# Decay columns made in the first batch, two more pairs transposed by DMA, and the last result in halves: a fused attention and MLP kernel

## The chip, the core and the metric

The kernel runs on one core of a Trainium2 chip. The metric is the time of one execution on the device, in microseconds (us). A core has TensorE (PE, with weight loads shown apart as PEld), VectorE (DVE), ScalarE (ACT), GpSimd (POOL) and SyncE (SP). SP computes nothing here; it issues most of the DMAs, one after the other and in program order. The profile gives one busy share for the core's 16 DMA engines, for all queues together.

## The reference, cut to what matters

Attention over 8 batches of 8 heads with 576 rows of 64 columns. The scores have a causal mask and a decay made from a running sum of `s`. Then an MLP with a hardswish between two matrices.

```python
scores = scale * np.matmul(q, k.transpose(0, 1, 3, 2))
s_pos = np.maximum(s, 0.0)
cum = np.cumsum(s_pos, axis=-1)
bias = -(cum[:, :, :, None] - cum[:, :, None, :])
scores = np.where(causal, -1e9, scores + np.minimum(bias, 0.0))
attn = softmax(scores)                       # written out in the original
x = np.matmul(attn, v)                       # then (B*S, H*D)
h = x @ w_in
out = (h * np.clip(h + 3.0, 0.0, 6.0) / 6.0) @ w_out
```

## The kernel before, where the change touches it

Heads go in 32 pairs. Scores need q and k transposed (the 64 columns on the partitions), with the decay as additional rows under them. Two ways exist side by side. Pairs below `PTD` are transposed on TensorE and copied by the DVE, and get their decay rows from a scratch tensor in memory (`load_aug`). Pairs from `PTD` on are laid out in SBUF with decay *columns* beside q and k, and one DMA transposes the whole.

```python
    PTD = 10
# ...
    def decay_columns():                      # all three parts, once, before pair 7
        for i in range(3):
            pD = psum.tile([128, NTR, NH], F16, tag="S", bufs=3, name="pD")
            for t in range(NTR + 1):          # ten small transposes
                nc.tensor.matmul(out=pD[r0:r1, j, :], lhsT=kaug[:, i, c:c + r1 - r0], ...)
            for r0, r1, j0, j1, h in (...):   # four DVE copies, eight for i == 0
                nc.vector.tensor_copy(out=dec[r0:r1, j0:j1, i, :], in_=src)
# ...
    def cast_columns(p):                      # POOL: q, k and the decay columns into xb
        nc.gpsimd.tensor_copy(out=..., in_=qk_f.pop(p))
        nc.gpsimd.tensor_copy(out=x[:, NTR:2 * NTR, D:D + 3], in_=dec[:, :, 0:3, p])
        nc.gpsimd.tensor_copy(out=x[:, 0:NTR, D + 3:D + 4], in_=dec[:, :, 3:4, p])

    def transpose_dma(p):                     # on the SP queue
        nc.sync.dma_start(out=qkT[:, p % NS, ...], in_=xb[:, p % 2]..., transpose=True)

    def load_pair(p):                         # also on the SP queue
        load_qk(p, nc.sync)
        load_v(p, nc.sync)
        if p < PTD:
            load_aug(p, nc.sync)
# ...
    def block0_tasks(p):                      # pairs 4 to 7, woven into the first MLP block
        def ahead():                          # look-ahead, after the pair's scores
            load_pair(p + 3)
            cast_qk(p + 1)
            cast_v(p + 1)
            # ...
        return (scores(2 * p) + scores(2 * p + 1)
            + [(ahead, 0), (lambda: attend(2 * p), 1200), (lambda: attend(2 * p + 1), 1200)]
            + transposes(p + 1) + [(lambda: x_transpose(p), 640)] + pause)
```

The last result is one PSUM bank of 512 columns (PSUM holds what TensorE writes), evicted, that is copied out and scaled, by the DVE in one instruction and stored by one DMA on SP.

The softmax here doesn't subtract the row's maximum and nothing guards it: scores larger than these inputs give would overflow.

## Time and profile before

| | before |
|---|---|
| time, median of 4 runs | 376.65 us (376.2 to 376.93) |
| span of the profiled run | 374.9 us |
| TensorE busy | 94% |
| first MLP matmul (end of the first batch) | 35.56 us |
| first scores of pairs 9, 10, 13 | 94.28, 101.91, 125.53 us |
| last eviction starts | 370.89 us |

The views used are these. The page has busy shares and a row of tenths per engine, 40 slices of the span. The timeline has one row per run of like instructions: start, length, engine, source line, operation, output <- inputs, count, and in brackets the idle time just ahead with what ended it. Rows of "SPq" are DMA issues: their length is how long the queue was held. A table by stretch gives busy time per engine, the granted TensorE clock, the mean busy share of the DMA engines, and GB/s. The page's account of the chain that ended last, and its row on the DMA transposes, complete what the prediction shows of this kernel:

```profile
PE 79%; DMA 8%; DVE 5%; ACT 4%; issue 2%; SPq 1%; POOL 1%; ACTq 0%; POOLq 0%
...
qkT<-xb SPq DMA_TRANSPOSE x22, 4.9
```

The chain is TensorE for four fifths of the span; DMA has the next largest part, 8%. 22 pairs take the DMA transpose, which lands 4.9 us after its issue.

### The profile page before, as it was taken

What the parts mean: (1) busy time and instruction counts of PE and PEld (TensorE: products, weight loads), DVE (VectorE), ACT (ScalarE), POOL (GpSimd) and SP (SyncE); (2) the same over time, 40 slices, a digit from 0 to 9 for tenths busy, and PEclk for the clock granted to TensorE, in tenths of its full rate; (3) what the DMA queues carried; (4) which work ended last, traced back from release to release, by engine and by line L of the source; (5) the groups of instructions that cost most, each with busy time, mean ns of one, the idle gap of its engine ahead of it and who ended that gap; (6) DMA issues with size and microseconds to landing.
All of it is one profiled execution on the core that took longest, in us unless ns stands there. A gap on an engine that the chain in (4) does not pass through costs nothing.

```text
span 374.9 us, 7607 instructions
## 1 busy us (share of the span) xinstructions
PE 354.1 (94%) x2784; PEld 219.6 (59%) x2784; DVE 190.9 (51%) x331; ACT 209.5 (56%) x404; POOL 148.9 (40%) x378
## 2 busy tenths in 40 slices
PE   6688979999999999999999999999999999999995
PEld 2465555556666566566656665666566656555542
DVE  5765855566652365345534553455345545554531
ACT  4464764336785677467746774677467714543310
POOL 5663335453666444444444444444445300000000
PEclk9989999999999999999999999999999999999999
DMA  9679999949799999998998989899995100010012
GB/s 161 138 155 203 191 212 211 229 118 194 147 205 204 231 219 198 202 235 189 187 235 180 199 183 233 191 191 185 219 188 113 49 29 36 22 56 30 28 58 84
DMA packets 184526, 59.36 MB, mean 158 GB/s; under 512 B 177840, under 2 KB 178064, under 8 KB 184488
## 3 DMA queue, kind: packets, MB, share of 16 engines
q1 hardware_dynamic: 182392, 54.42, 69.5%
q0 software_dynamic: 1680, 4.27, 6.3%
q8 instruction: 22, 0.36, 0.4%
q10 hardware_dynamic: 416, 0.19, 0.2%
q14 instruction: 16, 0.13, 0.1%
HBM read 37.49 MB, written 9.62 MB: 126 GB/s over the span
## 4 chain that ended last, share of the span: by engine, by line
PE 79%; DMA 8%; DVE 5%; ACT 4%; issue 2%; SPq 1%; POOL 1%; ACTq 0%; POOLq 0%
PE bank L423 25%; PE po L445 23%; PE S L291 9%; PE bank L445 8%; PE O L340 6%; PE bankS L423 4%; DMA qkT<-xb 3%; DMA qkT<-aug_scratch 3%; ACT Pm L299 2%; DMA qkf<-in_k_dram 1%; ACT trl L431 1%; DVE gT L432 1%; PE bank L465 1%; DMA s_sb<-in_s_dram 1%; DVE xs L352 1%
## 5 line engine op out<-in xcount | busy, mean ns | idle before, releaser
L299 ACT ACTIVATE Pm<-S 128x384 f16<-128x384 f32 (+2 forms) x256 | 115.5, 507 | 58.8 <-PE S L291 57.1
L432 DVE SCALAR_TENSOR_TENSOR gT<-trl,bank 128x512 f16<-128x512 f32 x123 | 84.5, 687 | 102.2 <-ACT trl L431 102.0
L304 POOL TENSOR_SCALAR_AFFINE_SELECT Pm<-Pm 128x128 f16<-128x128 f16 (+2 forms) x256 | 79.2, 311 | 132.6 <-ACT Pm L299 121.9
L431 ACT ACTIVATE trl<-bank,bias 128x512 f32<-128x512 f32 x123 | 85.2, 693 | 77.3 <-PE bank L423 75.3
L423 PE MATMUL bank<-xT,w_in 128*128 128x512 f16 x492 | 126.4, 382 | 0.7
L445 PE MATMUL po<-w_out_sb,gT 128*128 128x512 f16 x416 | 104.3, 379 | 0.0
L423 PEld LDWEIGHTS <-w_in 128*128 128x128 f16 x576 | 78.5, 146 | 32.9 <-issue 1.9
L445 PEld LDWEIGHTS <-gT 128*128 128x128 f16 x576 | 52.2, 98 | 48.6 <-issue 0.3
L291 PE MATMUL S<-qkT 128*128 128x320 f16 (+4 forms) x448 | 70.4, 263 | 8.0 <-ACT Pm L299 3.4
L291 PEld LDWEIGHTS <-qkT 128*128 128x128 f16 x448 | 41.3, 98 | 38.4 <-DVE qkT L262 4.5
L340 PEld LDWEIGHTS <-Pm 128*128 128x128 f16 x960 | 38.9, 98 | 13.2 <-POOL Pm L304 1.8
L340 PE MATMUL O<-v_h,Pm 128*128 128x65 f16 x960 | 41.4, 194 | 1.5 <-POOL Pm L304 1.3
L445 PE MATMUL bank<-w_out_sb,gT 128*128 128x512 f16 x160 | 39.4, 379 | 0.0
L352 DVE TENSOR_TENSOR xs<-O,r 128x640 f16<-128x640 f32 x32 | 26.4, 825 | 1.1
L454 DVE TENSOR_SCALAR osb<-po 128x512 f32<-128x512 f32 x26 | 17.9, 688 | 15.2 <-PE po L445 14.9
L222 POOL CAST xb<-qkf 128x1152 f16<-128x1152 f32 x22 | 25.3, 1149 | 0.0
L238 POOL CAST v_h<-v_f 128x640 f16<-128x640 f32 x28 | 20.1, 719 | 4.2 <-DMA v_f<-in_v_dram 4.2
L454 DVE TENSOR_SCALAR osb<-bank 128x512 f32<-128x512 f32 x10 | 6.9, 690 | 26.0 <-PE bank L445 26.0
L176 POOL CAST t<-qkf 128x1152 f16<-128x1152 f32 x10 | 11.5, 1146 | 13.1 <-DMA qkf<-in_k_dram 13.1
L423 PE MATMUL bankS<-xT,w_in 128*128 128x512 f16 x64 | 16.4, 379 | 0.0
L431 ACT ACTIVATE trl<-bankS,bias 128x512 f32<-128x512 f32 x16 | 11.0, 687 | 8.0 <-PE bankS L423 8.0
L432 DVE SCALAR_TENSOR_TENSOR gT<-trl,bankS 128x512 f16<-128x512 f32 x16 | 11.0, 689 | 6.8 <-ACT trl L431 6.8
(49 smaller groups left out, 122.7 us busy)
## 6 DMA issues: line engine op xcount, KB each, us to landing
qkf<-in_q_dram SPq DMA_DIRECT2D x32, 288.0 KB, 4.4
qkf<-in_k_dram SPq DMA_DIRECT2D x32, 288.0 KB, 4.1
out_dram<-osb SPq DMA_DIRECT2D x36, 256.0 KB, 2.7
v_f<-in_v_dram SPq DMA_DIRECT2D x64, 128.0 KB, 3.8
w_in<-in_moe_w_in_dram POOLq DMA_DIRECT2D x2, 1024.0 KB, 12.9
w_out_sb<-in_moe_w_out_dram POOLq DMA_DIRECT2D x4, 512.0 KB, 7.2
v_f<-in_v_dram SPq DMA_DIRECT2D x32, 32.0 KB, 2.7
qkT<-xb SPq DMA_TRANSPOSE x22, 4.9
```

Of the source, the lines that this page charges most:

```text
L222: nc.gpsimd.tensor_copy(out=x.rearrange("p (i t) c -> p t i c", i=2)[:, :, :, 0:D], in_=qk_f.pop(p))
L238: copy(out=v_h[:, sl, :, :, 0:D], in_=v_f[:, sl])
L291: nc.tensor.matmul(out=S[:, c:c + hi - lo], lhsT=kT[:, sl, off + 128 * kt:off + 128 * (kt + 1)], rhs=qT[:, sl, off + lo:off + hi], start=( ...
L299: nc.scalar.activation(out=P[:, p0:p0 + n], in_=S[:, 0:n], func=AF.Exp, scale=0.125, bias=0.0)
L304: nc.gpsimd.affine_select(out=view, in_=view, pattern=pattern, compare_op=ALU.is_ge, fill=0.0, base=0, channel_multiplier=-1,)
L340: nc.tensor.matmul(out=O[:, hh, qt * VW:qt * VW + D + 1], lhsT=P[:, c:c + 128], rhs=v_h[:, sl, hh, kt, 0:D + 1], start=(qt == 0), stop=(qt ...
L352: nc.vector.tensor_tensor(out=xs.rearrange("p t h d -> p h t d"), in0=Ov[:, :, :, 0:D], in1=r.to_broadcast([128, 2, 5, D]), op=ALU.mult,)
L423: nc.tensor.matmul(out=ph, lhsT=w_in_t[f // 8][:, kc, f % 8, :], rhs=xT[:, kc, n * 512:(n + 1) * 512], start=(kc == 0), stop=(kc == KC - 1),)
L431: nc.scalar.activation(out=trl, in_=ph, func=AF.Relu, bias=bias3[:, 0:1], scale=1.0)
L432: nc.vector.scalar_tensor_tensor(out=gT[n][:, f, :], in0=trl, scalar=6.0, in1=ph, op0=ALU.min, op1=ALU.mult)
L445: nc.tensor.matmul(out=po, lhsT=gT[n][:, f, t4 * 128:(t4 + 1) * 128], rhs=w_out_sb[:, f, :], start=(f == 0), stop=(f == NF - 1),)
L454: nc.vector.tensor_scalar_mul(out=osb, in0=po, scalar1=1.0 / 6.0)
```

## The change

The intent: make the decay columns early, where TensorE has gaps, so that pairs 8 and 9 can take the DMA transpose too and TensorE loses 18 transposes; and shorten what follows the last matmul.

```diff
-    PTD = 10
+    PTD = 8
@@ decay_columns: one part per call
-    def decay_columns():
-        for i in range(3):
-            pD = psum.tile([128, NTR, NH], F16, tag="S", bufs=3, name="pD")
+    def decay_columns(i):
+        pD = psum.tile([128, NTR, NH], F16, tag="M", bufs=2, name="pD")
             # ... the same matmuls and copies
@@ m2: the last of 36 results
+        if (n, t4) == (NBLK - 1, 3):
+            if part == 3:
+                last_result(n, t4)
+            return
@@
+    def last_result(n, t4):
+        for half, eng in enumerate((nc.sync, nc.scalar)):
+            # 16 matmuls of 256 columns, evicted by DVE (half 0) or ACT (half 1),
+            # stored from the queue eng
@@ first batch
-            t += [(lambda: x_transpose(p - 1), 640)]
+            t += [(lambda: x_transpose(p - 1), 640), (lambda: decay_columns(p - 1), 200)]
@@ block 0's look-ahead
-            load_pair(p + 3)
-            cast_qk(p + 1)
+            if p + 1 < PTD:
+                cast_qk(p + 1)
             cast_v(p + 1)
+            if p + 2 >= PTD:
+                cast_columns(p + 2)
+                transpose_dma(p + 2)
+            load_pair(p + 3)
             if p == 4:
                 load_w_out(3)
-            if p == 5:
                 load_columns()
@@
-        block0_tasks(6) + [(decay_columns, 640), (copy_columns, 0)] + block0_tasks(7),
+        [(copy_columns, 0)] + block0_tasks(6) + block0_tasks(7),
```

(`transposes(p + 1)` is left out for pair 8.)

More of the change, by code (lines that the diff above doesn't have):

```diff
@@ L186, in copy_columns @@
             nc.vector.tensor_copy(out=xb[:, i, :, 64:128], in_=xaug)
-    def decay_columns():
-        for i in range(3):
-            pD = psum.tile([128, NTR, NH], F16, tag="S", bufs=3, name="pD")
-            for t in range(NTR + 1):
-                r0, r1, c, j = (0, 128, 128 * t, t)
-                if t == 4:
-                    r1 = 64
-                elif t == 5:
-                    r0, c, j = 64, 0, 4
-                elif t > 5:
-                    c, j = 64 + 128 * (t - 6), t - 1
-                nc.tensor.matmul(
-                    out=pD[r0:r1, j, :],
-                    lhsT=kaug[:, i, c:c + r1 - r0],
-                    rhs=ident[0:NH, 0:NH],
-                    is_transpose=True,
-                    start=(t == 0),
-                    stop=(t == NTR),
-                )
-            pv = pD.rearrange("p t (a h) -> p t a h", h=2)
-            for r0, r1, j0, j1, h in (
-                (0, 128, 0, 4, 0), (0, 64, 4, 5, 0), (64, 128, 4, 5, 1), (0, 128, 5, 9, 1)
-            ):
-                src = pv[r0:r1, j0:j1, :, h]
-                nc.vector.tensor_copy(out=dec[r0:r1, j0:j1, i, :], in_=src)
-                if i == 0:
-                    nc.vector.tensor_scalar_mul(
-                        out=dec[r0:r1, j0:j1, 3, :], in0=src, scalar1=-1.0
-                    )
@@ new lines, in decay_columns @@
+    def decay_columns(i):
+        pD = psum.tile([128, NTR, NH], F16, tag="M", bufs=2, name="pD")
+        for t in range(NTR + 1):
+            r0, r1, c, j = (0, 128, 128 * t, t)
+            if t == 4:
+                r1 = 64
+            elif t == 5:
+                r0, c, j = 64, 0, 4
+            elif t > 5:
+                c, j = 64 + 128 * (t - 6), t - 1
+            nc.tensor.matmul(
+                out=pD[r0:r1, j, :],
+                lhsT=kaug[:, i, c:c + r1 - r0],
+                rhs=ident[0:NH, 0:NH],
+                is_transpose=True,
+                start=(t == 0),
+                stop=(t == NTR),
+            )
+        pv = pD.rearrange("p t (a h) -> p t a h", h=2)
+        for r0, r1, j0, j1, h in (
+            (0, 128, 0, 4, 0), (0, 64, 4, 5, 0), (64, 128, 4, 5, 1), (0, 128, 5, 9, 1)
+        ):
+            src = pv[r0:r1, j0:j1, :, h]
+            nc.vector.tensor_copy(out=dec[r0:r1, j0:j1, i, :], in_=src)
+            if i == 0:
+                nc.vector.tensor_scalar_mul(
+                    out=dec[r0:r1, j0:j1, 3, :], in0=src, scalar1=-1.0
+                )
@@ L456, in m2 @@
             nc.sync.dma_start(out=out[r0:r0 + 128, :], in_=osb)
+    def last_result(n, t4):
+        r0 = n * 512 + t4 * 128
+        osb = work.tile([128, 512], F32, tag="osb", bufs=3)
+        for half, eng in enumerate((nc.sync, nc.scalar)):
+            c0, c1 = half * 256, (half + 1) * 256
+            po = pouts[n, t4] if half == 0 else psum.tile([128, 512], F32, tag="Y", name="poL")
+            for f in range(NF):
+                nc.tensor.matmul(
+                    out=po[:, 0:256],
+                    lhsT=gT[n][:, f, t4 * 128:(t4 + 1) * 128],
+                    rhs=w_out_sb[:, f, c0:c1],
+                    start=(f == 0),
+                    stop=(f == NF - 1),
+                )
+            if half == 0:
+                nc.vector.tensor_scalar_mul(out=osb[:, c0:c1], in0=po[:, 0:256], scalar1=1.0 / 6.0)
+            else:
+                nc.scalar.mul(out=osb[:, c0:c1], in_=po[:, 0:256], mul=1.0 / 6.0)
+            eng.dma_start(out=out[r0:r0 + 128, c0:c1], in_=osb[:, c0:c1])
     bias3 = cpool.tile([128, 1], F32, tag="c_b3")
@@ L549, in ahead @@
         def ahead():
+            if p + 1 < PTD:
+                cast_qk(p + 1)
+            cast_v(p + 1)
+            if p + 2 >= PTD:
+                cast_columns(p + 2)
+                transpose_dma(p + 2)
             load_pair(p + 3)
-            cast_qk(p + 1)
-            cast_v(p + 1)
             if p == 4:
                 load_w_out(3)
-            if p == 5:
                 load_columns()
@@ L561, in block0_tasks @@
             + [(ahead, 0), (lambda: attend(2 * p), 1200), (lambda: attend(2 * p + 1), 1200)]
-            + transposes(p + 1)
+            + (transposes(p + 1) if p + 1 < PTD else [])
             + [(lambda: x_transpose(p), 640)]
```

## The prediction

> **What bounds the kernel now.** I read the head of the page first (busy shares, the 40 slices), then tables of busy time by stretch, then the timeline of TensorE with the idle time ahead of each row, and last the timeline of the SP queue. From the page:
>
> ```profile
> span 374.9 us, 7607 instructions
> PE 354.1 (94%) x2784; PEld 219.6 (59%) x2784; DVE 190.9 (51%) x331; ACT 209.5 (56%) x404; POOL 148.9 (40%) x378
> ...
> PE   6688979999999999999999999999999999999995
> ...
> DMA  9679999949799999998998989899995100010012
> ```
>
> TensorE is busy 94% and one slice is 9.4 us: from about 95 us on it is full, so what is removed from it there is a gain, unless a wait takes its place. Before 80 us it has gaps, and there the question is which wait ends last. In the DMA row the engines that move data are as full as TensorE up to 280 us, so a transpose that moves from TensorE to DMA moves from one busy resource to another.
>
> The table by stretch puts TensorE at 173.36 of 174 us between 126 and 300 us, at 38.79 of 40 between 86 and 126, and at only 20.11 of 26.8 between 8.5 and 35.3 us (the first batch, pairs 0 to 3). The timeline of TensorE shows what the three parts of the change touch: the first batch, the present decay columns, and the only later stall on a transposed load.
>
> ```profile
> 27.64 0.45 PE L378 MATMUL pTm<-ident,xs 128*128 128x128 f16 x5 [0.41 <-DVE xs L352]
> 28.29 0.63 PE L340 MATMUL O<-v_h,Pm 128*128 128x65 f16 x15 [0.19 <-DVE v_h L238]
> ...
> 56.60 0.54 PE L291 MATMUL S<-qkT 128*128 128x256 f16 x4 [1.13 <-DMA qkT<-aug_scratch]
> ...
> 73.29 0.66 PE L201 MATMUL pD<-ident,aug 64*128 64x64 f16 x10 [0.16 <-DVE qkT L262]
> 74.17 1.14 PE L201 MATMUL pD<-ident,aug 64*128 64x64 f16 x20 [0.23 <-DVE qkT L262]
> 75.25 1.04 PE L445 MATMUL po<-w_out_sb,gT 128*128 128x512 f16 x4
> 76.15 0.33 PE L291 MATMUL S<-qkT 128*128 128x256 f16 x2
> 77.12 0.84 PE L291 MATMUL S<-qkT 128*128 128x192 f16 x5 [0.64 <-ACT Pm L299]
> ...
> 125.53 0.56 PE L291 MATMUL S<-qkT 128*128 128x256 f16 x4 [0.57 <-DMA qkT<-xb]
> ```
>
> The brackets are idle time and its cause. The row at 56.60 is a wait on a load that is late by DMA traffic, not by TensorE; the row at 125.53 is pair 13 waiting for its transposed q and k. The SP queue tells why:
>
> ```profile
> 90.14 0.61 SPq L161 DMA_DIRECT2D v_f<-in_v_dram  x1
> 95.03 2.81 SPq L229 DMA_TRANSPOSE qkT<-xb  x1
> 97.95 1.22 SPq L370 DMA_TRANSPOSE xT<-xs  x1
> ...
> 119.40 2.87 SPq L229 DMA_TRANSPOSE qkT<-xb  x1
> ```
>
> Issuing one q/k transpose holds SP for 2.8 us. After an idle 4.3 us before 95.03 SP issues without a gap until 119.4: it needs 8.1 us per pair (95.03, 103.16, 111.35, 119.40) while TensorE in this stretch wants a pair every 7.5 us (94.28, 101.91, 109.41). So between 95 and 125 us the issuing of SP sets the end, and the start of that chain, the transpose of pair 10, decides when pair 13 can run.
>
> **What the Trainium skill says.** "DMA: Bandwidth & Descriptors", section "SWDGE vs HWDGE vs iDMA", ties the plain DMA transpose to the SP and ACT queues; here all 22 q/k transposes sit on SP, each 2.8 us of issue and 4.9 us to landing, so the two new ones queue ahead of other loads. The same page, "Issuing engines are not separate DMA queues", says that a second issuing engine saves only the issuer's time; so I give the tail little for its second queue (no run yet shows it). "TensorE: Matmul & The Clock Gate", "Part 4: PE-mode transpose", has about 275 ns for one 128x128 transpose in a kernel; the trace has a window of 219 ns, but nine of them advance TensorE by only 0.5 us (82.41 to 82.92), 56 ns each. I use 56. "Perfetto Trace Analysis", "Optimizing Tensor Performance", wants independent groups to rotate through PSUM banks so that evacuation overlaps; the new decay code rotates through only two, and below I find it waiting.
>
> **Part 1, decay columns out of the full stage.** TensorE leaves its previous work at 72.96 and starts the next at 75.25: 2.3 us. The three pD tiles also occupy all three S banks, so the next scores wait for their copies: I charge 0.4 of the 0.64 us idle at 77.12. **Removed: 2.7 us.** The DVE loses 16 copies here (12 at 235 ns, 4 at 230: 3.7 us), which do not bound.
>
> **Part 1, decay columns into the first batch.** Ten small matmuls each after x_transpose of pairs 0, 1 and 2, ahead of the next attend: 1.8/3 = 0.6 us each. They take banks M, of which there are two, in the order transposes g1, x_transpose, decay. So decay needs the bank that g1 of the same pair used, and must wait until the DVE has copied it. The DVE timeline has those copies ending at 23.2 us for pair 2 and at 29.0 for pair 3, where TensorE would otherwise start the attend at 22.40 and 28.29.
> - First: start at 23.2, attend at about 23.8, +1.4 us; of this a following idle 0.87 us (pair 3's q/k cast, itself waiting for a load) takes most, leaving +0.5.
> - Second: eight more DVE copies of the first (1.9 us) push g1's copies to about 29.6; attend at about 30.2 in place of 28.29: +1.9 in all.
> - Third: no bank wait, +0.6: **about +2.4 us at 35 us.**
>
> What of that survives: at 43.6 TensorE waits 0.2 us for the cast of pair 4, and at 56.6 1.13 us for pair 5's decay rows, issued at 45.73 and landing at 56.47 behind the weight loads. Neither depends on TensorE, so they swallow 1.3. **Left: +1.1 us.**
>
> **Part 2, pairs 8 and 9 by DMA.** Removed: 18 transposes at 56 ns, **1.0 us** of a full TensorE; 8 DVE copies (4 at 485, 4 at 421 ns, 3.6 us, beside other work); 2 loads of decay rows (0.44 us of SP each). Added: on POOL two pairs of small copies, 0.23 + 0.23 us each (the cast of 1.15 us replaces one of 1.14); on SP two issues of 2.8 us. The order changes too: the transpose now goes out ahead of load_pair, so SP waits for POOL's cast before it fetches the next pair. TensorE alone would then be 2.7 + 1.0 - 1.1 = 2.6 us early at 93 us.
>
> The SP chain, in times of the old trace plus the 1.1 us: POOL ends the cast for pair 8 at 73.4, SP is busy with the transpose to 76.2, q and k of pair 9 issued by 77.3 and landed some 4.2 us later (81.5), cast by 83.1, transpose to 86, loads of pairs 10 and 11 (3.5 us each, as at 81.97 to 90.75, with one store) to about 93.1; with the 1.1, 94.2 in place of 95.03. If the landing is quicker, 93.3. So the chain that ends in pair 13 moves by -0.8 to -1.7, not -2.6: **-1.2 us**; the rest becomes waiting for transposed q and k.
>
> **Part 3, the last result in halves.** TensorE's columns are the same: sixteen 512-column matmuls took 3.45 us; I expect two times sixteen of 256 to take as long, since in attend 15 weight loads with 65 columns pass in 0.47 us. At the end the ACT eviction of 256 columns replaces the DVE's 688 ns. ACT took 445 ns for 320 and 493 for 384 columns, so about 0.39: -0.3. The last DMA carries half of 256 KB; its landing was 1.9 us (371.6 to 373.5): an estimated -0.2. **-0.5 us.**
>
> **Sum:** -1.2 - 0.5 = -1.7, 374.9 us.
>
> **Rivals.** (a) The SP chain doesn't bind: pair 9's loads land early and pair 10's transpose follows TensorE. For it: the DMA row falls to 4 in the slice from 75 us, and SP idles 5.3 and 4.3 us at 75.8 and 90.8. Against it: the serial order transpose, load, cast, transpose. Then -2.6 - 0.5: 373.5. (b) The first batch costs all its 2.4 us, because a delay in POOL or ACT carries past the two DMA anchors; then TensorE gains only 1.3, and part of it goes to SP: 375.5 to 376.3. (c) The columns' copies, now ahead of pair 6, wait on the DVE for a 288 KB load sent at about 66 us, which would hold up its evictions. For it: the full DMA. Against it: the DVE has 4.3 us idle before 70.66, and I put the landing at 70 to 71. It would cost 0 to 1 us. (d) The gap removed at 73 to 77 us comes back as waits on exp and mask. Against it: ACT had been idle 6.9 us there.
>
> **Range and chances.** I give the SP chain 60%, (a) 25%, (b) with (c) 15%: 0.6 x 374.9 + 0.25 x 373.5 + 0.15 x 376 = 374.7; rounded towards (a), since a change made on purpose has its intent behind it, 374.6. The steps at worst add to about +0.5, at best (no cost in the first batch, no SP wait) to -4.2; so 372.4 to 376.9. Two per cent is 7.5 us, twice the best case: within 2% 0.96, faster 0.03, slower 0.01.
>
> **What would show it.** Right: decay matmuls at about 23, 29 and 34 us with idle before the first two put down to the DVE; the wait at 56.6 gone or near it; no pD near 73 us; q/k transposes on SP near 74.5 and 84; pair 10's near 94; more than 1 us of TensorE idle in all on transposed q/k between 95 and 126; a last eviction of about 0.4 us on ACT. Wrong: a decay batch without a wait, a stall on the DVE's column copies before 72 us, or TensorE reaching 126 us without waiting on a transpose, in which case (a) holds and the gain is 3 us or more.

## The result, and the profile after

The changed kernel took 378.49 us (median of 4 runs, 378.15 to 378.8) against 376.65 before: ratio 1.005, 95% interval 1.0032 to 1.0067. It is half a per cent slower, and above the top of the stated range. A ratio here is the mean time of one kernel's fast runs over the mean of the other's fast runs in the same rounds, so it isn't quite the ratio of the medians.

The same rows of the page as the prediction shows of before:

```profile
span 376.4 us, 7600 instructions
PE 355.6 (94%) x2782; PEld 220.9 (59%) x2782; DVE 186.1 (49%) x323; ACT 209.8 (56%) x405; POOL 150.0 (40%) x382
...
PE   7777979999798999999999999999999999999996
...
DMA  9689999499899999999999999999994200001012
```

TensorE's eleventh and thirteenth slices (94 to 103 and 113 to 122 us) are down to 7 and 8, and the hole in the DMA row (the 4) has moved from the ninth slice (75 to 85 us) to the eighth (66 to 75). What opens the hole there turns out to be the cause: a transpose that waits, with loads behind it. A hole as such says little: the kernel before has two of some 4 us in the same stretch (78 to 82 and 92 to 96 us) and is faster. The timeline of TensorE, rows with idle time that answer to those of before:

```profile
23.04 0.65 PE L200 MATMUL pD<-ident,aug 64*128 64x64 f16 x10 [0.73 <-DVE qkT L261]
...
29.00 0.65 PE L200 MATMUL pD<-ident,aug 64*128 64x64 f16 x10 [0.71 <-DVE qkT L261]
...
58.07 0.72 PE L290 MATMUL S<-qkT 128*128 128x192 f16 x4 [0.55 <-DVE qkT L261]
...
101.94 0.72 PE L290 MATMUL S<-qkT 128*128 128x256 f16 x6 [2.13 <-DMA qkT<-xb]
...
118.94 0.56 PE L290 MATMUL S<-qkT 128*128 128x256 f16 x4 [1.35 <-DMA qkT<-xb]
```

The decay matmuls wait for the DVE twice, as foreseen. New are 2.13 us ahead of pair 10's scores and 1.35 ahead of pair 12's, both on the DMA that transposes q and k. The way of TensorE through the two kernels, at places that exist in both:

| place on TensorE | before | changed | shift |
|---|---|---|---|
| first MLP matmul | 35.56 | 37.39 | +1.8 |
| first scores of pair 6 | 65.45 | 66.88 | +1.4 |
| first MLP matmul of block 1 | 85.79 | 83.80 | -2.0 |
| first scores of pair 9 | 94.28 | 92.16 | -2.1 |
| first scores of pair 10 | 101.91 | 101.94 | 0.0 |
| first scores of pair 12 | 116.10 | 118.94 | +2.8 |
| first scores of pair 13 | 125.53 | 127.65 | +2.1 |
| last eviction starts | 370.89 | 373.04 | +2.2 |
| end of the span | 374.9 | 376.4 | +1.5 |

TensorE was 2.1 us ahead at pair 9 and lost 4.2 us by pair 13; from there nothing moves until the tail. The two waits are 3.5 us of it; in this trace TensorE's granted clock also fell, to 0.66 and 0.50 of full speed, between 102 and 106 us (see the last section). The SP queue of the changed kernel shows where it went:

```profile
68.83 0.54 SPq L460 DMA_DIRECT2D out_dram<-osb  x1
74.53 2.80 SPq L228 DMA_TRANSPOSE qkT<-xb  x1
77.39 0.57 SPq L148 DMA_DIRECT2D qkf<-in_q_dram  x1
...
84.79 2.69 SPq L228 DMA_TRANSPOSE qkT<-xb  x1
87.53 0.58 SPq L148 DMA_DIRECT2D qkf<-in_q_dram  x1
...
93.36 3.10 SPq L157 DMA_DIRECT2D v_f<-in_v_dram  x2
96.50 0.61 SPq L161 DMA_DIRECT2D v_f<-in_v_dram  x1
97.22 2.74 SPq L228 DMA_TRANSPOSE qkT<-xb  x1
```

From 69.4 to 74.5 SP issues nothing. It stands at pair 8's transpose, whose source POOL finishes at 74.5, and the loads of pair 9 stand behind it. In the kernel before, those loads went out from 70.60. The table by stretch shows what the DMA engines did meanwhile (the last two figures of a row are their busy share, which this view can put above 1, and GB/s):

```profile
70.00:72.00 2.00, 2.00 (x37) 1.41 (x36) 0.06 (x1) 0.95 (x3) 1.74 (x5) 1.00 0.33 124
72.00:74.00 2.00, 2.00 (x18) 1.17 (x17) 1.97 (x4) 0.00 (x0) 2.00 (x3) 1.00 0.00 0
74.00:76.00 2.00, 1.89 (x17) 0.99 (x15) 1.80 (x5) 0.46 (x2) 0.51 (x3) 1.00 0.06 14
```

Nothing moved for nearly 4 us. So pair 9's q and k came late, and POOL, which casts them, waited:

```profile
83.28 1.15 POOL L221 CAST xb<-qkf 128x1152 f16<-128x1152 f32 x1 [2.65 <-DMA qkf<-in_k_dram]
...
92.50 1.15 POOL L221 CAST xb<-qkf 128x1152 f16<-128x1152 f32 x1 [1.60 <-DMA qkf<-in_k_dram]
```

These are pairs 9 and 10. Pair 9's transpose went out at 84.8, the loads of pairs 10 and 11 crowded in after it, and pair 10's transpose left at 97.2, 2.2 us later than before the change. For comparison, the start of pair 10's loads in the kernel before, and its `v` loads for pair 11 (in the changed kernel those at 93.36, 3.10 us long):

```profile
81.97 0.39 SPq L148 DMA_DIRECT2D qkf<-in_q_dram  x1
...
88.42 1.67 SPq L157 DMA_DIRECT2D v_f<-in_v_dram  x2
```

The tail did what it should. First the last eviction of before:

```profile
370.89 0.69 DVE L454 TENSOR_SCALAR osb<-bank 128x512 f32<-128x512 f32 x1 [2.76 <-PE bank L445]
```

And of the changed kernel:

```profile
373.04 0.38 ACT L479 ACTIVATE osb<-poL 128x256 f32<-128x256 f32 x1 [13.17 <-PE poL L469]
373.45 0.38 ACTq L480 DMA_DIRECT2D out_dram<-osb  x1
```

From the start of the last eviction to the end of the span is 4.0 us before and 3.4 after.

### The profile page after: what moved, and what is told of

Its sections match the earlier page's. It is cut to its first block, busy times and chain, and to the rows that moved or that the text cites. A ratio compares the mean times of both kernels' runs of the same rounds, so it can differ in the third digit from the quotient of the medians.

```text
span 376.4 us, 7600 instructions
## 1 busy us (share of the span) xinstructions
PE 355.6 (94%) x2782; PEld 220.9 (59%) x2782; DVE 186.1 (49%) x323; ACT 209.8 (56%) x405; POOL 150.0 (40%) x382
## 4 chain that ended last, share of the span: by engine, by line
PE 80%; ACT 5%; DVE 5%; DMA 5%; issue 2%; SPq 1%; POOL 0%; ACTq 0%; POOLq 0%
PE bank L422 26%; PE po L449 23%; PE S L290 10%; PE bank L449 8%; PE O L339 7%; PE bankS L422 4%; ACT Pm L298 3%; DMA qkT<-xb 2%; DVE gT L431 2%; ACT trl L430 2%; DVE qkT L261 1%; DMA amask<-amask 1%; PE bankY L422 1%; DVE xs L351 1%; PE pT L377 1%
## 5 line engine op out<-in xcount | busy, mean ns | idle before, releaser
L422 PE MATMUL bank<-xT,w_in 128*128 128x512 f16 x492 | 127.7, 385 | 1.0 <-DVE gT L431 0.2
L449 PEld LDWEIGHTS <-gT 128*128 128x128 f16 x560 | 50.8, 98 | 47.0 <-issue 0.7
L449 PE MATMUL bank<-w_out_sb,gT 128*128 128x512 f16 x144 | 35.8, 379 | 0.0
L221 POOL CAST xb<-qkf 128x1152 f16<-128x1152 f32 x24 | 27.6, 1152 | 4.2 <-DMA qkf<-in_k_dram 4.2
L349 DVE RECIPROCAL r<-O 128x10 f32<-128x10 f32 x32 | 6.9, 216 | 14.0 <-PE O L339 13.9
```

The source lines that it names most:

```text
L221: nc.gpsimd.tensor_copy(out=x.rearrange("p (i t) c -> p t i c", i=2)[:, :, :, 0:D], in_=qk_f.pop(p))
L422: nc.tensor.matmul(out=ph, lhsT=w_in_t[f // 8][:, kc, f % 8, :], rhs=xT[:, kc, n * 512:(n + 1) * 512], start=(kc == 0), stop=(kc == KC - 1),)
L449: nc.tensor.matmul(out=po, lhsT=gT[n][:, f, t4 * 128:(t4 + 1) * 128], rhs=w_out_sb[:, f, :], start=(f == 0), stop=(f == NF - 1),)
```

## The experiments

**Theory.** The order on the SP queue costs the time: a transpose that waits for POOL holds up the loads behind it, the DMA engines stand idle, and the late loads delay the transposes of pairs 9 and 10, from which the chain to pair 13 hangs. **Rivals:** the DMA engines or SP are simply full with two more transposes; or the cost lies in the first batch. All twelve runs gave correct results. "Kernel before" in the tables was run in the same rounds on the same chip; chips differ, and the first and the last one scattered (the kernel before from 374.9 to 379.9 and from 374.9 to 380.3).

| kernel | median us | before, us | ratio (95% interval) |
|---|---|---|---|
| loads first in both look-aheads | 375.39 | 376.6 | 0.9951 (0.9900 to 1.0002) |
| pairs 8, 9 on TensorE again | 375.04 | 376.6 | 0.9948 (0.9903 to 0.9994) |
| kernel before, last result in halves | 375.36 | 376.6 | 0.9969 (0.9921 to 1.0018) |
| changed, decay in bank Y | 377.0 | 376.6 | 1.0002 (0.9956 to 1.0048) |
| changed, unaltered | 378.76 | 376.08 | 1.0061 (1.0036 to 1.0087) |
| loads first for pair 6 only | 374.99 | 376.08 | 0.9963 (0.9940 to 0.9986) |
| loads first for pair 7 only | 378.15 | 376.08 | 1.0064 (1.0039 to 1.0090) |
| loads first and bank Y | 371.83 | 376.08 | 0.9886 (0.9863 to 0.9908) |
| loads first in both, again | 373.65 | 375.5 | 0.9951 (0.9932 to 0.9971) |
| bank Y, pairs 8, 9 on TensorE | 372.96 | 375.5 | 0.9931 (0.9918 to 0.9945) |
| loads first, bank Y, no halves | 372.48 | 375.5 | 0.9928 (0.9904 to 0.9952) |
| changed, loads of 9, 10 on ACT | 373.46 | 376.18 | 0.9929 (0.9874 to 0.9983) |

### The loads first

```diff
+            load_pair(p + 3)
             if p + 1 < PTD:
                 cast_qk(p + 1)
             cast_v(p + 1)
             if p + 2 >= PTD:
                 cast_columns(p + 2)
                 transpose_dma(p + 2)
-            load_pair(p + 3)
```

> The changed kernel, with load_pair again ahead of the casts and of the DMA transpose in block 0's look-ahead, as in the kernel before; nothing else differs. Theory (the order on the SP queue): in the changed kernel SP stands still from 69.4 to 74.5 us for POOL's cast of pair 8 while the DMA engines carry nothing from 72 to 76 us, so pair 9's q and k come late, POOL waits for them 2.65 us, and pair 10's transpose is issued at 97.2 in place of 95.0. With the loads first, pair 9's loads go out near 70, its transpose near 82, pair 10's near 92 to 93; TensorE's waits of 2.13 and 1.35 us on transposed q and k near 102 and 119 us go or shrink below 1 us in all; time 374.5 to 376, that is 2.5 to 4 us less than the changed kernel. Rival (the DMA engines or SP are simply full with two more transposes): pair 10's transpose stays near 96 to 97 and the time within 0.7 us of 378.5. Rival (the cost lies in the first batch): no change of the time either, above 378.

Four lines moved. The SP queue of this run:

```profile
68.54 0.38 SPq L148 DMA_DIRECT2D qkf<-in_q_dram  x1
...
74.66 2.88 SPq L228 DMA_TRANSPOSE qkT<-xb  x1
...
83.88 2.89 SPq L228 DMA_TRANSPOSE qkT<-xb  x1
...
92.47 2.72 SPq L228 DMA_TRANSPOSE qkT<-xb  x1
```

And the table by stretch:

```profile
70.00:72.00 2.00, 2.00 (x36) 1.45 (x36) 0.00 (x0) 1.08 (x3) 1.74 (x5) 1.00 1.21 260
72.00:74.00 2.00, 2.00 (x18) 1.08 (x15) 1.90 (x4) 0.00 (x0) 2.00 (x3) 1.00 0.89 171
```

Pair 8's transpose leaves when it did, but pair 9's loads now fill the idle stretch, pair 10's transpose leaves at 92.5 in place of 97.2, and no wait of TensorE on transposed q and k is left. The last eviction starts at 368.12 (373.04 in the changed kernel). The times of this chip scattered by 2 us, so the kernel was run again on another:

> The loads first in both look-aheads, nothing else, again: on the first chip the runs spread over 2 us and the interval reached 1.000. Theory: 0.993 to 0.997 of the kernel before. If it comes out at 1.000 or above, the gain seen in the first trace was chance.

It gave 0.9951 with an interval of 0.9932 to 0.9971, pair 10's transpose at 92.95. The gain stands: by the ratios about 1.1% under the changed kernel (0.9951 over 1.0061), with the same number of transposes and bytes. That the DMA engines or SP are full falls.

### Which of the two look-aheads

The changed kernel ran beside these two as the measure.

> The changed kernel unaltered, on the chip of this call, as the measure for the other runs of the call. Expected 1 to 2.5 us slower than the kernel before, with waits on transposed q and k near 102 and 119 us.

It was 2.7 us slower than the kernel before by the medians, a little more than expected, with waits on transposed q and k of 1.65, 0.55, 1.64 and 1.36 us at pairs 10 to 13.

```diff
+            if p == 6:              # second kernel: 7
+                load_pair(p + 3)
             # ... casts, transpose
-            load_pair(p + 3)
+            if p != 6:              # second kernel: 7
+                load_pair(p + 3)
```

> The changed kernel with load_pair ahead of the casts and the transpose only in the look-ahead of pair 6 (so pair 9's loads go ahead of pair 8's transpose), pair 7's look-ahead as changed. Theory (the first hold-up on SP, from 69 to 74.5 us with idle DMA engines, starts the chain): pair 8's transpose still near 74.5, pair 9's near 82 to 83 in place of 84.8, pair 10's near 93 in place of 97.2; nearly all of the gain of 3 us or so that both orders gave. Rival (the second hold-up, at pair 7, is what matters): pair 10's transpose at 96 or later and at most 1 us gained.

Transposes at 74.81, 82.36 and 92.95, and 374.99 us, 3.8 less than the changed kernel: all as the theory said. Two waits remain, 1.08 and 0.69 us, at pairs 12 and 13. From this run's SP queue:

```profile
82.36 2.68 SPq L228 DMA_TRANSPOSE qkT<-xb  x1
85.10 0.58 SPq L148 DMA_DIRECT2D qkf<-in_q_dram  x1
...
92.95 3.53 SPq L228 DMA_TRANSPOSE qkT<-xb  x1
```

Pair 10's transpose is 4.3 us earlier than in the changed kernel. Of this 2.4 us come from pair 9's transpose, and 1.8 from the loads of pairs 10 and 11 with the store: from their start to pair 10's transpose it is 7.9 us here and 9.7 there.

> The mirror image: load_pair first only in the look-ahead of pair 7, pair 6's as changed. Theory: POOL still waits about 2.6 us for pair 9's q and k near 81 us; pair 10's loads go out 2 us earlier, pair 9's transpose about 2 us later (87), pair 10's near 95: about half of the gain, 1 to 2 us under the changed kernel. Rival (pair 7's order is what matters): as fast as with both orders.

POOL waited the expected 2.65 us and pair 9's transpose left at 87.39, as expected. But pair 10's left at 96.16 rather than 95, waits of 1.07, 1.88, 0.47 and 0.84 us stayed, and the ratio (1.0064) is that of the changed kernel. I had expected half of the gain and there is none to be seen beyond the noise: once pair 9's loads are late, the order behind them matters little.

### The same order, another queue

Here the program keeps the changed order; only the queue of two pairs' loads differs.

```diff
     def load_pair(p):
-        load_qk(p, nc.sync)
-        load_v(p, nc.sync)
+        eng = nc.scalar if p in (9, 10) else nc.sync
+        load_qk(p, eng)
+        load_v(p, eng)
         # ... load_aug likewise; pairs 9 and 10 have none
```

> The changed kernel with its own order of the program, but the loads of pairs 9 and 10 are issued on the ACT queue, so they can't stand behind the transposes of pairs 8 and 9 on SP; bytes, transposes and DMA engines are the same. Theory (standing in line on SP): pair 9's loads leave near 71 to 74 us in place of 77.4, pair 9's transpose is issued near 82 to 83 in place of 84.8, pair 10's near 92 to 94 in place of 97.2, the waits on transposed q and k near 102 and 119 us go or fall below 1 us in all, and the time falls by 2.5 us or more against the changed kernel: 0.994 to 0.998 of the kernel before. Rival (DMA bandwidth, or the order of POOL's casts): within 1 us of the changed kernel, 1.003 or more.

Pair 9's first load on the ACT queue, and pair 10's transpose on SP:

```profile
70.03 0.46 ACTq L148 DMA_DIRECT2D qkf<-in_q_dram  x1
```

```profile
91.94 2.60 SPq L228 DMA_TRANSPOSE qkT<-xb  x1
```

No wait on a transpose is left in TensorE's timeline, and the last eviction starts at 367.60. The interval is wide (0.9874 to 0.9983), but it lies wholly under that of the changed kernel. The loads first and the loads on ACT are different edits. They have in common that the loads of pairs 9 and 10 no longer stand behind the transposes of pairs 8 and 9, and they give the same cure. This run alone could owe its gain to the issuing that it takes off SP, but the loads first take none off. With the run for pair 6 only, where just pair 9's loads go ahead, I take standing in line on SP as shown.

### Pairs 8 and 9 on TensorE

```diff
-    PTD = 8
+    PTD = 10
```

> The changed kernel with pairs 8 and 9 transposed on TensorE again (decay columns still made in the first batch, last result still in halves). Theory (the two added transposes and their order cost it): the first batch still costs 1.4 us at 67 us, the decay columns removed from the full stage give 2.9, the tail 0.7: 374 to 375.5. Rival (the first batch costs it): 377.5 or more.

375.04 us and 0.9948: the decay columns in the first batch and the halves are by themselves a small gain (the interval reaches 0.9994), so the first batch is not by itself what made the change slower. The wait of before for pair 13 is back at 0.63 us.

### The first batch: another bank

```diff
-        pD = psum.tile([128, NTR, NH], F16, tag="M", bufs=2, name="pD")
+        pD = psum.tile([128, NTR, NH], F16, tag="Y", name="pD")
```

> The changed kernel with the decay columns' PSUM tile in the bank Y, which nothing else uses in the first batch, in place of the two banks M. All theories: the idle 0.73 and 0.71 us ahead of the decay matmuls near 23 and 29 us go. Theory (the SP chain is paced by POOL's cast of pair 8, which follows TensorE): the gain is carried to the end, up to 1.4 us, so 377 to 378. Rival (a wait for pair 5's decay rows near 56 us swallows it): pair 6's first scores stay near 66.9 us and the time at 378.5.

The two idle times ahead of the decay matmuls are gone, and in the trace the last eviction starts at 371.58, 1.5 us earlier than in the changed kernel. Pair 10's transpose, at 95.30, moved by 1.9. The time (377.0) is in the expected range, but this chip's scatter makes the ratio inconclusive. With the loads first as well:

> Both repairs: the loads first in both look-aheads and the decay columns' tile in bank Y. Theory: the two gains add, since with the loads first TensorE is the bound again: 1.4 us under the run with the loads first alone, so 4 to 5 us under the changed kernel and 2 to 3 under the kernel before (0.992 to 0.994 of it); TensorE ends near 366.7 us in its trace. Rival (after the SP order is mended a wait elsewhere takes bank Y's share): within 0.5 us of the loads first alone.

371.83 us, 0.9886 (0.9863 to 0.9908): the best version, 1.1% under the kernel before and, by the medians of that chip, 1.8% under the changed one. The first decay group now follows at once:

```profile
21.39 0.66 PE L200 MATMUL pD<-ident,aug 64*128 64x64 f16 x10
```

There is no bracket, so no idle. The last eviction starts at 366.32, against 368.12 and 368.61 in the two runs with the loads first alone: 1.8 to 2.3 us, more than the 1.4 of the two waits. Part of the difference is luck: the granted clock between 8.5 and 36 us was 1.00 in this trace and 0.94 in the two others.

> Decay columns in the first batch in bank Y, pairs 8 and 9 transposed on TensorE as before, last result in halves. Theory (with the SP order mended, the DMA transposes save about the 1.0 us that 18 transposes of 56 ns take): 0.5 to 1.5 us slower than both repairs with pairs 8 and 9 by DMA (371.8 on the chip before), so 0.990 to 0.993 of the kernel before. Rival (the DMA transposes still cost, only less): as fast or faster than that version, 0.989 or less.

0.9931 (0.9918 to 0.9945), last eviction at 367.76. So once the loads don't stand in line, taking pairs 8 and 9 off TensorE is worth 1.4 us in the traces, and some 1.7 us by the ratios (0.0045 of 376; the two kernels ran on different chips, and also differ in the place of `load_pair` in the look-ahead). The 18 transposes at 56 ns account for 1.0; the rest is not settled.

### The last result in halves

```diff
 # the kernel before, with last_result and its call added as in the change
```

> The kernel before with only the last result in two halves. Every theory: TensorE ends at the same time within 0.1 us, the time after its end falls from 4.0 to about 3.4 us; 0.5 to 0.8 us faster than the kernel before, 375.8 to 376.1. If the second queue or the halved matmuls cost something, nothing or slower.

In the trace 374.3 - 370.95 = 3.4 us follow the start of the last eviction, against 4.0: the tail is worth its 0.6 us, and the halved matmuls take no longer. The time, 0.9969 with an interval that reaches 1.0018, can't confirm it on this chip. The counter-test:

> Both repairs, the last result in one piece as in the kernel before. Every theory: TensorE ends at the same time, the tail after it is 4.0 in place of 3.4 us; 0.5 to 0.8 us slower than both repairs with the halves, so about 0.990 to 0.991 of the kernel before. The run of the tail alone was lost in that chip's spread.

0.9928 (0.9904 to 0.9952): slower than with the halves (0.9886) by some 1.6 us, more than the 0.6 expected; but the chips differ and the two intervals overlap a little (0.9904 to 0.9908), so the times don't settle it. In the traces the tail is 4.0 us here (370.2 - 366.18) and 3.4 with the halves (369.7 - 366.32).

## Why the prediction was wrong, point by point

- **What bounds it:** right. Full TensorE, and between 95 and 125 us the chain on SP that starts with pair 10's transpose. The prediction put 30.5 us from that issue to pair 13's scores (95.03 to 125.53); in the changed kernel it is 127.65 - 97.22 = 30.4.
- **Decay columns removed, 2.7 us:** right. Between pair 6 and block 1 the shift goes from +1.4 to -2.0; with 0.5 for pair 8's nine transposes, 2.9 are left.
- **Decay columns in the first batch, +2.4 us:** the two waits came as told (0.73 and 0.71 us), the size was +1.8, since the second group's bank was free by 29.0 despite the extra copies.
- **"What of that survives", +1.1:** +1.4, for another reason. The wait of 1.13 us on pair 5's decay rows was gone, but 0.55 and 0.36 us of waits on the DVE stood in its place, so only 0.4 was swallowed, not 1.3. Two errors nearly cancel here, 0.6 us too much cost and 0.9 too much swallowed; that is luck.
- **TensorE 2.6 us early at 93 us:** 2.1 at pair 9. Up to here the sum holds to half a microsecond.
- **The SP chain: the step that failed.** The mechanism was right and one term of its sum was too small. The prediction had seen that "SP waits for POOL's cast before it fetches the next pair" and followed it: pair 8's transpose at 74.5 (measured 74.53), pair 9's at 84.2 (84.79). Then it gave the loads of pairs 10 and 11, with one store, 7.1 us of SP, at the rate of the old trace; they took 9.6 (87.53 to 97.11), 2.5 us of the 3.0 by which the chain came late. So pair 10's transpose left at 97.2 in place of "94.2", and "-0.8 to -1.7" became +2.1 at pair 13. When pair 9's loads are not held up the two pairs go through nearly at the old rate (7.8 us in the run for pair 6 only; pair 11's in 3.6 us with the loads first, 5.3 in the changed kernel). My reading is crowding: the old rate followed 4 us in which nothing moved (78 to 82 us), while in the changed kernel the traffic held up earlier came on top, from 76 us on without a break. That is argued, not shown: what exactly held SP for 3.10 us in pair 11's `v` loads is not settled by the trace.
- **The tail, -0.5:** -0.65.
- **Rivals:** (a), that the chain doesn't bind, was wrong for this kernel, yet is just what the reordered kernels show. (b), that the first batch costs all its 2.4 us, did not occur either in that size: it took 1.8, of which 1.4 were left at pair 6. (c), the columns' copies on the DVE, did not occur: the load landed in 3.2 us and the copies ran at 67.7 with 3.2 us of idle DVE behind them. (d) did not occur either. Moving the figure towards (a) because a change made on purpose has its intent behind it was no evidence, and went the wrong way.
- **The sum:** with +2.1 for the chain in place of -1.2, and -0.65 for -0.5, it would have been +1.5, which is the difference of the two spans.

## What to carry to other kernels

A DMA that waits at the head of an in-order queue holds up everything behind it (here SP, from 69.4 to 74.5 us). Put the loads that wait for nothing ahead of a DMA whose source an engine has yet to make, or on another queue. Where the DMA engines carry nothing, ask whether a load that could have gone, and is needed soon, stands behind such a wait; the hole alone doesn't tell (the faster kernel before had two). When you move a piece of work into an early stage with idle time, give its PSUM tile a bank that nothing else takes turns in there (bank Y removed two waits of 0.7 us). And when you predict a chain, leave a margin on a rate that comes from a stretch with different traffic around it: 7.1 us became 9.6.

## What the Trainium skill lacked or had wrong

- "DMA: Bandwidth & Descriptors", "Issuing engines are not separate DMA queues", says that DMAs from several engines only save the issuer's time. It lacks that a DMA that waits also holds up those behind it on its queue, so that a second queue can save more than the time of issuing: moving the loads of two pairs to the ACT queue, with the same bytes, took the ratio from 1.006 to 0.993.
- No page gives the time that a transpose of this size holds the queue on this chip: 128x2304 fp16, SBUF to SBUF, held SP for 2.7 to 3.8 us (median 2.8, changed kernel) and landed 4.8 us after issue (median), where a plain load of 288 KB held it for 0.4 to 0.6 us when nothing was in its way.
- "TensorE: Matmul & The Clock Gate", "Part 4: PE-mode transpose", has about 275 ns per 128x128 transpose in one kernel. The window here is 219 ns, but in a row they cost 56 ns each (nine in 0.5 us), and taking away 18 of them, with their copies, gained 1.4 us in the traces.
- The same page, "Why this matters for your kernels", warns of idle gaps over about 3 us. In the trace of the changed kernel the clock fell after a gap of 2.13 us, as these stretches show (the third figure from the end is the granted clock):

```profile
102.00:104.00 2.00, 2.00 (x10) 1.09 (x11) 0.00 (x0) 1.36 (x3) 0.89 (x3) 0.66 0.73 166
104.00:106.00 2.00, 2.00 (x7) 0.91 (x6) 0.69 (x1) 1.40 (x3) 0.49 (x3) 0.50 1.27 251
```

That the gap alone did it is not shown. A second trace of the same kernel, with a gap of 1.65 us there, kept 1.00, and so did the run for pair 7 only after 1.88 us. The slower clock seems to have cost little in the end: in that second trace waits on the transposes took its place, the transposes of pairs 10 to 13 left at nearly the same times (97.14 to 121.75 us, against 97.22 to 122.07), and the times on the two chips are alike (378.5 and 378.8).
